# A fused retention and SoLU kernel: new instruction orders on every engine, and some casts and scales on other engines

## The chip, the cores and the metric

The kernel runs on one core of one Trainium2 chip. The metric is the device time of one execution, in microseconds (us). A profiled execution of the same program gives a trace with the start and duration of each instruction on each engine. PE is the engine that multiplies matrices, DVE the vector engine, ACT the scalar engine, POOL the GpSimd engine, and SP the engine that here only issues loads and stores.

## The reference

```python
# retention: q, k, v are (8, 8, 576, 64); B = batch, H = heads, S = positions, D = 64
scores = 1/sqrt(D) * q @ k^T
gamma = 1 - 2**(-5 - head);  Dmat = gamma**(i - j) where i >= j, else 0
attn = (scores * Dmat) @ v                      # (8, 8, 576, 64)
x = attn.transpose(0, 2, 1, 3).reshape(4608, 512)
# SoLU block: w_in (512, 1024), w_out (1024, 512), g_ln (1024)
h = x @ w_in
solu = h * softmax(h)
ln = (solu - mean) / sqrt(var + 1e-6) * g_ln
out = ln @ w_out                                # (4608, 512) float32
```

## The kernel before

The 576 positions of a batch are cut into two windows of 256 and a tail of 64. The tails of four batches make one window together, so there are 18 windows of 256 rows. A window is worked in two halves of four heads, which gives 36 steps `i` of retention, and in two tiles of 128 rows, which gives 36 tiles `t` of the SoLU block. Matrices are float16 on PE, sums float32.

A step `i` consists of these operations; the name of each is the letter(s) with the step's number:

- `ldq`, `ldk`, `ldv` (SP): the loads of 256 KB each; in the tails each is four transfers of 64 KB. There are five buffers for each of q, k and v.
- `sq`, `sk`: the scaling of q and k by powers of gamma, with the cast to float16 (`scale`, L394); `cv`: the cast of v (`cast_v`, L399). Each of these may stand on DVE, ACT or POOL, as the table `ON` says.
- `T` (PE): transposes of q and k (`qk_tp`, L419 wide, L429 in small tiles); `Te` or `TL` (ACT): their copy to SBUF (L455, L457). `TL` takes the transposes of step `i` together with those of an `L`.
- `K` (PE): k^T v of the step (`kv_mm`); `st` (DVE), `sm` and `sc` (POOL, L562 and L571): the running state of a batch, its decay and its cast.
- `S` (PE): the scores (`scores`, L508), into PSUM bank `s`; `mask` (DVE, L540).
- `I` (PE): the part of the output that comes from the state (`inter`); `V` (PE): the part from the masked scores (`av`); both into bank `xy`, L472. `xe` (ACT, L576): the copy to x.

A tile `t` consists of `M1` (PE, x @ w_in, L587, into bank `h`), `ex` (ACT, exp, L595), `so` (DVE, the product h * e, which frees bank `h`, L610), `bnA`, `bnB` (DVE, the variance), `fx` (ACT) and `rs` (POOL, 1/sqrt for a window, L650), `L` (PE, transposes of the product, L439 wide, L446 small), `Le` or `TL` (ACT), `M2` (PE, times w_out, L660), `oe` (ACT, the scaled result, L669, which frees the bank of `M2`, mostly `s`) and `out` (SP, the store). There are three buffers between `oe` and `out`. PE's steady group is `I L T V K S M1 M2`, each with its own number; the `M2` in it is four tiles behind the `M1`.

The weights come in eight transfers of 512 KB: `lwi0` to `lwi3` for w_in, cast in halves by `wi0a` to `wi3b` (L706), and `lwo0`, `lwo2`, `lwo4`, `lwo6` for w_out, scaled by g_ln in `wg0` to `wg7` (DVE L710, ACT L714). `WM` (PE, L720) makes the column means of all eight scaled blocks, after which `wc0` to `wc7` (DVE, L728) subtract them. `M2_0` needs all `wc`.

The order of the work is written out by hand. The tables `FIRST` and `LAST` list, for each engine, the operations of the first some twenty steps and of the last few; in between, an operation's place on its engine comes from a due time, its period (4.92 us a step) plus an offset. `order_ops` merges the engines' lists into one program order with the durations of `DUR`; each engine works through its own list strictly in turn and waits at the head of it. SP's list is a queue too: a store that waits for its `oe` holds the loads that stand behind it. Each transfer also waits until the one eight before it is complete.

Where the plan leaves PE idle before `M2_0`, `fill` puts in matmuls on zeros (L846) that keep it busy: 33 of them in this kernel, beside 12 at the start.

```python
q = o.name[0] in "VKSTL" and not wide(o.name)
x += 0.1 if q != quad else 0.0     # a change between small and whole tiles on PE
```

Of the kernel before, what the change touches and what calls it, by code (L numbers as in the profile page):

```python
# [9 lines left out]
FP = mybir.dt.float32  # L10
# [3 lines left out]
P = 128  # L14
# [3 lines left out]
for _b in range(0, B, 4):  # L18
# [5 lines left out]
    T=0.26, L=0.26, Tw=0.45, Lw=0.45, I=0.22, V=0.23, K=0.13, S=0.22, M1=1.73, M2=1.73, M2h=0.87, oeh=0.42, G=0.1, WM=1.73,  # L24
    TL=1.03, Te=0.58, Le=0.58, xe=0.74, ex=1.22, oe=0.69, va=1.25, wiA=0.62, wiB=0.45, wg=0.68, wgD=0.43,
    cvA=0.62, mask=1.22, st=0.58, so=1.22, soA=1.3, bnA=0.68, bnB=0.89, fx=0.2, fin=0.42, wc=0.74, wm=0.62,
    sqD=0.75, gc=0.17, cvD=0.45, sq=1.04, sk=1.04, cv=0.61, sm=0.42, sc=0.81, rs=0.69, rsB=1.0,
    ldx=0.88, ldw=1.36, out=0.65,
)
HOP, PE_OUT = 0.07, 0.2  # L30
# [4 lines left out]
ON = {'sq0': 'DVE', 'sq1': 'DVE', 'cv0': 'ACT', 'cv1': 'ACT', 'sk2': 'DVE', 'sk3': 'DVE', 'cv2': 'ACT', 'cv3': 'ACT', 'cv4': 'ACT', 'cv5': 'ACT', 'cv6': 'ACT', 'cv7': 'ACT'}  # L35
CAP = dict(
    rawq=5, rawk=5, rawv=5, q16=3, k16=4, v16=4, ev=8, s=1, ret=2, xy=1, gg=6, gt=2, s160=4, s161=9, h=1,
    e=2, solu=4, osb=3, tl=1, tlx=2, tlT=1, tlL=1, wst=5,
# [3 lines left out]
FIRST = dict(  # L42
    PE=(
# [5 lines left out]
    ),  # L49
    ACT=(  # L50
# [4 lines left out]
    ),  # L55
    DVE=(
# [5 lines left out]
    ),  # L62
    POOL=(
# [4 lines left out]
    ),  # L68
    SP=(
# [47 lines left out]
def wide(name):  # L117

    return name[0] == "T" and int(name[1:]) < NJ + 2 or name[0] == "L" and int(name[1:]) < NJ - 4


def plan():
    ops = []
    rank = {n: x - 1e4 for lst in FIRST.values() for x, n in enumerate(lst.split())}
    rank.update({n: x + 1e4 for lst in LAST.values() for x, n in enumerate(lst.split())})

# [5 lines left out]
    for i in range(NS):  # L132
# [32 lines left out]
    for t in range(NT):
# [5 lines left out]
        op(f"so{t}", "DVE", "soA" if va else "so", [f"ex{t}"], (m, 4.56), [("solu", [f"L{t}", f"va{t}" if va else f"bnB{t}"])])  # L171
# [5 lines left out]
        if c:  # L177
# [6 lines left out]
        after = [f"Te{NJ + 1}", f"Le{t - 1}"] if t == NJ - 4 else [f"TL{NS - 3}"] if t + 4 == NS - 2 else []  # L184
        after += [f"Le{t - 2}"] if t - 2 >= NS - 6 else []
        op(f"L{t}", "PE", "Lw" if early else "L", [f"so{t}"] + after, (m + 2, 0.1),
           [("tlL" if early else "tl" if jn else "tlx", [ev_L(t)])])
        if not jn:
# [3 lines left out]
        op(f"M2_{t}", "PE", "M2h" if end else "M2", need, (t + LAG, 3.1), [("h" if end else "xy" if late(t) and t % 2 else "s", [f"oe{t}"])])  # L192
# [5 lines left out]
    for c in range(4):  # L198
        op(f"lwi{c}", "SP", 0.47, [], (-4, 0.5 + 0.1 * c), [("wst", [f"wi{c}a", f"wi{c}b"])], DUR["ldw"])
        op(f"wi{c}a", "ACT", dict(ACT="wiA", DVE="wiB"), [f"lwi{c}"], (1, 0.1 * c))  # L200
        op(f"wi{c}b", "DVE", dict(ACT="wiA", DVE="wiB"), [f"lwi{c}"], (1, 0.1 * c))
    for c in range(0, 8, 2):
        op(f"lwo{c}", "SP", 0.47, [], (-2, 0.6 + 0.1 * c), [("wst", [f"wc{c}", f"wc{c + 1}"])], DUR["ldw"])
        for x in (c, c + 1):
            op(f"wg{x}", "DVE" if x % 2 else "ACT", dict(DVE="wgD", ACT="wg"), [f"lwo{c}", "gc"], (1, 1.0 + 0.1 * x))
            op(f"wc{x}", "DVE", "wc", ["wm" if WE else "WM", f"lwo{c}"], (4, 0.1 * x))
    op("G", "PE", "G", [], (-9999, 0.0), [("h", ["gc"])])
# [15 lines left out]
def parts(name):  # L223

    if name[:2] == "lw":
        return 1
    n = int(name[3:])
    if WINS[n // 2][1] == 2:
        return 2 if name[:3] == "out" else 4
# [731 lines left out]
```

## Time and profile before

| | us |
|---|---|
| median of 3 runs (lowest, highest) | 212.61 (212.51, 213.25) |
| span of the profiled execution, first to last instruction | 210.9 |
| PE busy, with the matmuls on zeros | 200.8 |
| DVE busy | 166.1 |
| ACT busy, POOL busy | 141.7, 141.7 |

Of the profiled execution's own time only the span is given; what lies around the span, up to the runs' median, is 1.7 us. In a row of the timeline the first number is the start, the second the duration, then engine, line, operation, the tensors written and read, shapes and count; in brackets stands the idle time of the engine just before, and what ended it. In a table of stretches each engine has its busy time and instruction count, followed by the granted clock of PE, the busy share of the DMA engines and the rate. A row of a group has the busy time and the mean duration in ns behind the first bar, and the idle time before its instructions behind the second.

### The profile page before, as it was taken

What the parts mean: (1) busy time and instruction counts of PE and PEld (TensorE: products, weight loads), DVE (VectorE), ACT (ScalarE), POOL (GpSimd) and SP (SyncE); (2) the same over time, 40 slices, a digit from 0 to 9 for tenths busy, and PEclk for the clock granted to TensorE, in tenths of its full rate; (3) what the DMA queues carried; (4) which work ended last, traced back from release to release, by engine and by line L of the source; (5) the groups of instructions that cost most, each with busy time, mean ns of one, the idle gap of its engine ahead of it and who ended that gap; (6) DMA issues with size and microseconds to landing.
All of it is one profiled execution on the core that took longest, in us unless ns stands there. A gap on an engine that the chain in (4) does not pass through costs nothing. (4 is left out here: it accounts for less than half of the span.)

```text
span 210.9 us, 10171 instructions
## 1 busy us (share of the span) xinstructions
PE 200.8 (95%) x4400; PEld 113.2 (54%) x4400; DVE 166.1 (79%) x279; ACT 141.7 (67%) x235; POOL 141.7 (67%) x240
## 2 busy tenths in 40 slices
PE   7986989999999999999999999999999999999992
PEld 2442654665566555555555555555666555554451
DVE  6565779997868898978898898889988998753760
ACT  2375787897666776776666777666767777573752
POOL 7434758999997975948787979797979792001110
PEclk9999999999999999999999999999999999999999
DMA  5999999999666559778999686776355222311224
GB/s 157 345 355 334 329 311 269 301 293 306 195 188 188 169 139 278 217 214 259 314 288 305 198 252 183 217 234 181 94 152 153 54 57 67 71 63 54 101 101 104
DMA packets 64814, 42.66 MB, mean 202 GB/s; under 512 B 3320, under 2 KB 58624, under 8 KB 64768
## 3 DMA queue, kind: packets, MB, share of 16 engines
q1 hardware_dynamic: 64528, 41.82, 68.4%
q8 instruction: 34, 0.56, 1.2%
q10 hardware_dynamic: 240, 0.18, 0.5%
q14 instruction: 12, 0.10, 0.2%
HBM read 32.55 MB, written 9.44 MB: 199 GB/s over the span
## 5 line engine op out<-in xcount | busy, mean ns | idle before, releaser
L587 PE MATMUL h_ps<-w_in,xT 128*128 128x512 f16 x288 | 68.5, 380 | 0.0
L660 PE MATMUL o_ps<-w2c,ev 128*128 128x512 f16 (+1 forms) x296 | 67.6, 373 | 0.0
L610 DVE TENSOR_TENSOR solu<-h_ps,e_sb 128x1024 f16<-128x1024 f32 x32 | 39.2, 1223 | 16.7 <-ACT e_sb L595 16.5
L595 ACT ACTIVATE e_sb<-h_ps 128x1024 f32<-128x1024 f32 x36 | 36.8, 1023 | 21.9 <-PE h_ps L587 20.4
L540 DVE TENSOR_TENSOR ret<-s_ps,masks 128x1024 f16<-128x1024 f32 x36 | 43.9, 1220 | 6.0 <-PE s_ps L508 5.4
L660 PEld LDWEIGHTS <-ev 128*128 128x128 f16 x296 | 28.7, 98 | 32.7
L616 DVE BATCH_NORM_STATS2 bs<-solu 128x6 f32<-128x512 f16 x64 | 43.6, 685 | 0.9
L587 PEld LDWEIGHTS <-xT 128*128 128x128 f16 x288 | 25.3, 98 | 29.1 <-ACT xT L576 0.8
L394 POOL TENSOR_TENSOR q<-rawq,small 128x512 f16<-128x512 f32 x34 | 35.4, 1042 | 7.3 <-DMA rawq<-in_q_dram 5.9
L669 ACT ACTIVATE o_sb<-o_ps,rs 128x512 f32<-128x512 f32 (+1 forms) x37 | 25.0, 676 | 21.8 <-PE o_ps L660 10.4
L394 POOL TENSOR_TENSOR k<-rawk,small 128x512 f16<-128x512 f32 x34 | 35.4, 1042 | 6.0 <-DMA rawk<-in_k_dram 5.9
L457 ACT COPY ev<-tl 128x1024 f32<-128x1024 f32 (+1 forms) x32 | 29.7, 932 | 4.7 <-PE tl L429 4.2
L576 ACT CAST xT<-xy 128x512 f16<-128x512 f32 x36 | 26.7, 742 | 3.0 <-PE xy L472 2.9
L571 POOL CAST sbd<-gg 64x256 f16<-64x256 f32 x64 | 25.4, 397 | 3.0
L562 POOL TENSOR_TENSOR gg<-gt,small 128x128 f32<-128x128 f32 x32 | 13.1, 409 | 16.9 <-DVE gt L557 16.5
L648 POOL TENSOR_TENSOR w<-mv,w 128x2 f32<-128x2 f32 x16 | 3.1, 194 | 27.8 <-ACT w L633 13.9
L399 POOL CAST v<-rawv 128x512 f16<-128x512 f32 x28 | 17.1, 609 | 0.2
L508 PE MATMUL s_ps<-ev 64*64 64x128 f16 x576 | 14.8, 218 | 0.3
L472 PE MATMUL xy<-ret,v 64*64 64x128 f16 x576 | 14.7, 217 | 0.0
L472 PEld LDWEIGHTS <-sbd 128*128 128x128 f16 x128 | 9.3, 98 | 9.3 <-issue 1.1
L446 PE MATMUL tl<-ident,solu 64*64 64x64 f16 x1024 | 14.2, 195 | 0.0
L846 PE MATMUL tl<-zeros 128*128 128x512 f16 x41 | 12.7, 445 | 1.3 <-DVE zeros L802 1.3
(71 smaller groups left out, 214.6 us busy)
## 6 DMA issues: line engine op xcount, KB each, us to landing
rawq<-in_q_dram SPq DMA_DIRECT2D x32, 256.0 KB, 5.1
rawk<-in_k_dram SPq DMA_DIRECT2D x32, 256.0 KB, 5.3
rawv<-in_v_dram SPq DMA_DIRECT2D x32, 256.0 KB, 5.1
out_dram<-o_sb SPq DMA_DIRECT2D x26, 256.0 KB, 3.1
out_dram<-o_sb SPq DMA_DIRECT2D x19, 128.0 KB, 2.3
wst<-in_moe_w_in_dram SPq DMA_DIRECT2D x4, 512.0 KB, 6.8
wst<-in_moe_w_out_dram SPq DMA_DIRECT2D x4, 512.0 KB, 7.1
rawq<-in_q_dram SPq DMA_DIRECT2D x16, 64.0 KB, 2.4
```

The lines of the kernel that those rows point to most:

```text
L394: eng.tensor_tensor(out=t.rearrange("p j h d -> p h j d"), in0=st[i]["r" + nm], in1=g, op=ALU.mult)
L457: nc.scalar.copy(out=t[:, lo:hi].rearrange("p x (r w) -> p r x w", r=2), in_=tls[n].rearrange("p r x w -> p (r x w)").bitcast(FP).rearrang ...
L472: nc.tensor.matmul(start=(c, e) not in begun, stop=False, skip_group_check=True, **kw)
L540: nc.vector.tensor_tensor(out=d["ret"].rearrange("p e h j q -> p (e h) (j q)"), in0=d["s"].rearrange("p e h j q -> p (e h) (j q)"), in1=ma ...
L571: nc.gpsimd.tensor_copy(out=t[ee[e], :, :, ee[e]], in_=st[i]["gg"][ee[e]])
L576: nc.scalar.copy(out=xT[:, 2 * w : 2 * w + 2, 2 * hf : 2 * hf + 2].rearrange("p c h (q j) -> p c h j q", j=2), in_=xys[i][:, :, 0:256].rea ...
L587: nc.tensor.matmul(out=h_ps[:, hh], lhsT=xT[:, t, dc], rhs=w_in16[:, dc, hh], start=(dc == 0), stop=(dc == 3),)
L595: nc.scalar.activation(out=d["e"], in_=d["h"], func=ACT.Exp, accum_out=se[:, t : t + 1])
L610: nc.vector.tensor_tensor(out=d["solu"], in0=d["h"], in1=d["e"], op=ALU.mult)
L616: nc.vector.bn_stats(out=d["bs"][:, half], in_=d["solu"][:, half * 512 : half * 512 + 512])
L660: nc.tensor.matmul(out=o, lhsT=d["ev"][:, d["lo"] + c], rhs=w2c16[:, c, mm], start=(c == 0), stop=(c == 7))
L669: nc.scalar.activation(out=d["osb"][:, mm], in_=d["o", half], func=ACT.Copy, scale=ws[t // 2]["rs"][:, t % 2 : t % 2 + 1])
```

## The change

The change does four things that reach the program.

1. `FIRST` and `LAST` go; a table `ORDER` lists all operations of all engines from the first to the last step. The planner's durations, its load queue and its rule for DVE and POOL at the same time are other ones, and by them the merged program order and the place of the matmuls on zeros (34 instead of 33).
2. `ON` moves operations: `sk0 sq2 sq3 sq4 sk6 cv9 sq11 cv11` from POOL to DVE; `sq1 sk3` from DVE to POOL; `cv1 cv3 cv4 cv6` from ACT to POOL; `cv14` from POOL to ACT; of the weights `wi0a wi1a wi2a` from ACT to POOL, `wi3a wg0 wg4` from ACT to DVE, `wi1b wg5 wg7` from DVE to ACT.
3. On SP the loads and stores have another order. Of the first 34 transfers the same ones stand in places 1 to 25 and 26 to 34, but inside them `lwo0` goes from the 18th place to the 25th and `ldv6` from the 25th to the 19th. Later, loads run ahead of their numbers, and some stores behind later ones (`out3 ldk17 ldq17 out2 out4`, `out13 out12`, `out19 ldq31 ldq35 out18`, `out25 out23 out24`).
4. On PE every step keeps its operations and the same ones stand ahead of `M1_4`, but `I V K L T S` change places within a group. `L2` comes before `T9`.

Small: the table of constants has 94 columns instead of 78; the buffers of the weights are a pool of their own at the end. The diff also brings transposes by DMA, split loads, a second bank for the end and extra load buffers, but their switches (`LX`, `TX`, `R0`, `OT`, `SPL`) are set so that none of them is used.

```diff
-HOP, PE_OUT = 0.07, 0.2
+HOP, PE_OUT = 0.04, 0.2
...
-ON = {'sq0': 'DVE', 'sq1': 'DVE', 'cv0': 'ACT', 'cv1': 'ACT', 'sk2': 'DVE', 'sk3': 'DVE', 'cv2': 'ACT', 'cv3': 'ACT', 'cv4': 'ACT', 'cv5': 'ACT', 'cv6': 'ACT', 'cv7': 'ACT'}
+ON = {'sq0': 'DVE', 'sq1': 'POOL', 'cv0': 'ACT', 'cv1': 'POOL', 'sk2': 'DVE', 'sk3': 'POOL', 'cv2': 'ACT', 'cv3': 'POOL', 'cv4': 'POOL', 'cv5': 'ACT', 'cv6': 'POOL', 'cv7': 'ACT', 'sk0': 'DVE', 'wi3a': 'DVE', 'sq2': 'DVE', 'sq3': 'DVE', 'sq4': 'DVE', 'sk6': 'DVE', 'wg4': 'DVE', 'wg0': 'DVE', 'cv9': 'DVE', 'sq11': 'DVE', 'cv11': 'DVE', 'wi1b': 'ACT', 'wg5': 'ACT', 'wg7': 'ACT', 'cv14': 'ACT', 'wi1a': 'POOL', 'wi0a': 'POOL', 'wi2a': 'POOL'}
...
+LX = ()
+TX = ()
+R0 = 99
+OT = 99
+SPL = ()
...
-FIRST = dict(
+ORDER = dict(
     PE=(
-        "T0 S0 K0 K1 T1 I0 S1 V0 I1 V1 M1_0 K2 T2 T3 K3 S2 M1_1 I2 S3 V2 L0 I3 V3 T4 L1 K4 S4 M1_2 K6 WM K5 "
-        "M1_3 T5 K7 T6 I4 S5 V4 T7 I5 S6 V5 T8 M1_4 I6 S7 V6 K8 T9 L2 M2_0 I7 L3 V7 K9 S8 M1_5 M2_1 I8 L4 V8 "
-        "K10 S9 T10 M1_6 M2_2 I9 L5 V9 S10 K11 T11 M1_7 M2_3 I10 L6 V10 S11 K12 T12 M1_8 M2_4 I11 L7 T13 V11 "
...
+        "G T0 K0 K1 S0 T1 S1 I0 V0 I1 V1 M1_0 K2 T2 S2 T3 M1_1 K3 S3 T4 I2 V2 L0 I3 V3 S4 K4 M1_2 K6 L1 WM K5 M1_3 T5 K7  "
+        "S5 T6 I4 V4 T7 I5 V5 S6 T8 M1_4 I6 S7 V6 K8 L2 T9 M2_0 I7 L3 V7 S8 K9 M1_5 M2_1 I8 V8 L4 K10 T10 S9 M1_6 M2_2  "
+        "I9 V9 K11 L5 T11 S10 M1_7 M2_3 I10 V10 K12 L6 T12 S11 M1_8 M2_4 I11 L7 V11 K13 T13 S12 M1_9 M2_5 I12 V12 L8 T14  "
...
     DVE=(
-        "wg3 mask4 st6 so2 st5 wc4 wc0 wc7 wc1 st7 so3 mask5 wc5 wc2 wc6 mask6 wc3 mask7 fin0 st8 so4 mask8 "
-        "st9 bnA4 fin1 so5 bnA5 mask9 bnB4 st10 so6 bnB5 mask10 st11 so7 bnA7 mask11 bnB7 st12 bnA6 so8 "
...
+        "sk0 sq0 gc st0 mask0 st1 mask1 wi3b wi0b wi3a wi2b sk2 sq2 sq3 so0 st2 mask2 sq4 st3 mask3 so1 sk6 wg4 st4  "
+        "mask4 wg3 wg1 wg0 st6 so2 wc1 st5 wc0 wc2 wc3 st7 wc6 mask5 so3 wc5 wc4 mask6 wc7 mask7 st8 fin0 cv9 so4 fin1  "
+        "mask8 st9 sq11 bnA4 so5 cv11 mask9 st10 bnA5 so6 bnB5 mask10 st11 bnA6 so7 bnB4 mask11 bnA7 st12 so8 bnB7  "
...
     POOL=(
-        "sk0 sk1 sm0 sc0 sm1 sc1 sq2 sq3 sm2 sc2 sm3 sc3 sk4 sq4 sk6 sm4 sc4 sk5 sm6 sk7 sm5 sq5 sc5 sq6 sq7 "
-        "sk8 sq8 sk9 sc6 cv8 sq9 sm7 sc7 rs0 sq10 cv9 sq11 sm8 cv11 sk10 sc8 cv10 sk11 rs1 sm9 sc9 sq12 sm10 "
...
+        "sk1 cv1 sq1 sm0 sc0 sm1 sc1 wi1a wi0a wi2a sk3 cv3 sm2 sk4 sc2 sm3 sc3 cv4 cv6 sm4 sc4 sk5 sm6 sk7 sq5 sm5 sc5  "
+        "sq6 sq7 sk8 sq8 sc6 cv8 sq9 sk9 sm7 sc7 rs0 sm8 sc8 sk10 cv10 sq10 sm9 sc9 sq12 sk11 sm10 rs1 sq13 cv12 sc10  "
...
     SP=(
-        "ldq0 ldk0 ldv0 ldv1 ldq1 ldk1 lwi1 lwi2 lwi0 lwi3 ldk2 ldv2 ldq2 ldk3 ldq3 ldv3 lwo4 lwo0 ldk4 ldq4 "
-        "ldv4 lwo6 ldk6 lwo2 ldv6 ldk5 ldv5 ldk7 ldq5 ldv7 ldq6 ldk8 ldq7 ldq8 ldk9 ldv8 ldq9 ldq10 ldv9 "
...
+        "ldk0 ldq0 ldk1 ldv0 ldv1 ldq1 lwi3 lwi1 lwi0 lwi2 ldk2 ldv2 ldq2 ldq3 ldk3 ldv3 ldk4 ldq4 ldv6 ldv4 lwo4 ldk6  "
+        "lwo6 lwo2 lwo0 ldk5 ldv5 ldk7 ldq5 ldv7 ldq6 ldq7 ldk8 ldq8 ldv8 ldq9 ldk9 ldv9 ldq10 ldv11 ldv10 ldk10 ldq12  "
+        "ldq11 ldq13 out0 ldk11 ldk12 ldq14 ldq16 ldv12 ldq15 ldv14 ldv13 ldv15 out1 ldv16 ldk13 ldk14 ldk15 out3 ldk17  "
+        "ldq17 out2 out4 ldk16 out5 ldq20 ldv18 ldk18 ldk19 out6 ldk20 ldq21 ldq19 ldk21 ldv17 ldq18 ldv20 out7 ldv19  "
...
-    rank = {n: x - 1e4 for lst in FIRST.values() for x, n in enumerate(lst.split())}
-    rank.update({n: x + 1e4 for lst in LAST.values() for x, n in enumerate(lst.split())})
+    rank = {n: x for lst in ORDER.values() for x, n in enumerate(lst.split())}
...
-        t = max(free[o.eng], lock if o.eng == "POOL" else free["POOL"] if locks(o) else 0.0)
+        t = free[o.eng]
...
         if locks(o):
+            if free["POOL"] > x + 0.05:
+                end += 0.2
+                free["POOL"] += 0.18
             lock = end
+        elif o.eng == "POOL" and lock > x + 0.05:
+            end += 0.18
...
+            u = units(o.name) / np
             for _ in range(np):
-                end = max([end + o.dur / np] + landed[-7:-6])
+                begin, end = end, end + o.dur / np
+                held += u
+                while held > 5.0:
+                    held -= landed[out_at][1]
+                    end = max(end, landed[out_at][0] - 0.2)
+                    out_at += 1
```

More of the change, by code (lines that the diff above doesn't have):

```diff
@@ L183, in plan @@
         early = t < NJ - 4
[L184 to L188, printed above, removed]
+        if t in LX:
+            op(f"lx{t}", "SP", "lx", [f"so{t}"], (m + 2, 0.1), [("ev", [f"M2_{t}"])], DUR["ltx"])
+        lasts = [x for x in range(NT) if NJ - 4 <= x < OT and ev_L(x)[:2] == "Le"]
+        after = [f"Te{NJ + 1}", f"Le{NJ - 5}"] if t == NJ - 4 else []
+        if t in lasts:
+            after += [f"Le{t - 2}" if t - 2 in lasts else ev_T(max(i for i in range(NS) if i not in TX))]
+        if t not in LX:
+            op(f"L{t}", "PE", "Lw" if wide(f"L{t}") else "L", [f"so{t}"] + after, (m + 2, 0.1),
+               [("tlL" if early else "o2" if t >= OT else "tl" if jn else "tlx", [ev_L(t)])])
+        if ev_L(t)[:2] == "Le":
             op(f"Le{t}", "ACT", "Le", [f"L{t}"], (m + 2, 0.95), [("ev", [f"M2_{t}", "M3" if t == NT - 1 else ""])])
@@ L191, in plan @@
         need = [ev_L(t)] + [f"wc{x}" for x in range(8)] + ["cs" if t == NT - 2 else ""]
-        op(f"M2_{t}", "PE", "M2h" if end else "M2", need, (t + LAG, 3.1), [("h" if end else "xy" if late(t) and t % 2 else "s", [f"oe{t}"])])
+        if t == OT:
+            need += [ev_T(max(x for x in range(NS) if x not in TX)), ev_L(max(x for x in range(OT) if x not in LX))]
+        op(f"M2_{t}", "PE", "M2h" if end else "M2", need, (t + LAG, 3.1), [(home(t), [f"oe{t}"])])
         op(f"oe{t}", "ACT", "oeh" if end else "oe", [f"M2_{t}", f"rs{w}"], (t + LAG + 1, 0.1), [("osb", [f"out{t}"])])
@@ L223, in parts @@
 def parts(name):
-    if name[:2] == "lw":
+    if name[:2] in ("lw", "lx"):
         return 1
+    if name[:2] == "tx":
+        return 2
     n = int(name[3:])
+    if name[:2] == "ld" and split(n) and name[2] != "q":
+        return 4
     if WINS[n // 2][1] == 2:
@@ L230, in parts, with units @@
     return 2 if name[:3] == "out" and 22 <= n < 28 else 1
+def units(name):
+    if name[:3] == "out":
+        return 0.25
+    if name[:2] in ("lw", "lx", "tx"):
+        return dict(lw=0.5, lx=2.0, tx=4.0)[name[:2]]
+    return 2.0 if split(int(name[3:])) and name[2] != "q" else 1.0
 def order_ops(ops):
@@ L303, in _np_table @@
         st[64 * (h % 2) : 64 * (h % 2) + 64, h // 2] = gam[h] ** 256.0
-    small = np.concatenate(cols + [st, np.ones((P, 1)), np.full((P, 1), -0.5), np.eye(P, 8)], 1)
+    pos_s = 128 * (p[:, None] // 64) + 64 * j[None] + p[:, None] % 64
+    ks = (gam[None, :, None] ** (128.0 - pos_s[:, None, :])).reshape(P, 16)
+    small = np.concatenate(cols + [st, np.ones((P, 1)), np.full((P, 1), -0.5), np.eye(P, 8), ks], 1)
     return small.astype(np.float32)
@@ L339 @@
     pool("raw", CAP["rawq"])
-    for name in ("q16", "k16", "v16", "ev", "ret", "gg", "gt", "e", "solu", "osb", "wst"):
+    for name in ("q16", "k16", "v16", "ev", "ret", "gg", "gt", "e", "solu", "osb"):
         pool(name, CAP[name])
@@ L376, in load @@
         hh = slice(4 * hf, 4 * hf + 4)
-        st[i]["r" + nm] = t = pools["raw"].tile([P, 4, 2, D], FP, tag=nm, name="raw" + nm)
-        if wi < 2:
+        if extra(i) and "bis" not in pools:
+            loads_w.close()
+            pool("bis", CAP["bisq"])
+        st[i]["r" + nm] = t = pools["bis" if extra(i) else "raw"].tile([P, 4, 2, D], FP, tag=nm, name="raw" + nm)
+        if split(i) and nm != "q":
+            for n in range(4):
+                r0 = 256 * wi + 64 * n
+                nc.sync.dma_start(
+                    out=t[64 * (n // 2) : 64 * (n // 2) + 64, :, n % 2],
+                    in_=src[b, hh, r0 : r0 + 64, :].rearrange("h p d -> p h d"),
+                )
+        elif wi < 2:
             nc.sync.dma_start(
@@ L400, in cast_v, with bank @@
         st[i]["v16"] = t
+    def bank():
+        if "o2" not in pools:
+            banks_2.close()
+            pool("o2", CAP["o2"], space=PS)
+        return pools["o2"].tile([P, 512], FP, tag="o2", name="o_ps")
     def tl_of(n):
@@ L503, in scores @@
         qT, kT = qk_of(i, 0), qk_of(i, 1)
+        sz = s_ps.rearrange("p e h j q -> p e h (j q)")
         for hp in range(2):
@@ L507, in scores @@
                     for e in range(2):
+                        half = split(i) and j
+                        qq = slice(64 * c + 32, 64 * c + 64) if half else ee[c]
+                        oo = sz[ee[c], e, hp, 128:192] if half else sv[ee[c], e, hp, j]
                         nc.tensor.matmul(
-                            out=sv[ee[c], e, hp, j], lhsT=kT[ee[e], hp, j, ee[c]],
-                            rhs=qT[ee[e], hp, :, ee[c]], start=True, stop=True,
+                            out=oo, lhsT=kT[ee[e], hp, j, ee[c]], rhs=qT[ee[e], hp, :, qq], start=True, stop=True
                         )
@@ L654, in mm2 @@
         d = tk[t]
-        nm = "xy" if half or late(t) and t % 2 else "s"
-        nm = "h" if t == NT - 1 and not half else nm
+        nm = "xy" if half else home(t)
         mm = slice(256 * half, 256 * half + (256 if t == NT - 1 else DM))
-        d["o", half] = o = pools[nm].tile([P, 2, 512], FP, tag=nm, name="o_ps")[:, 0, 0 : mm.stop - mm.start]
+        o = bank() if nm == "o2" else pools[nm].tile([P, 2, 512], FP, tag=nm, name="o_ps")[:, 0]
+        d["o", half] = o = o[:, 0 : mm.stop - mm.start]
         for c in range(8):
@@ L867 @@
                 emit(o)
+    if "bis" not in pools:
+        loads_w.close()
+    pool("gu", 1)
     def general(t):
```

167 lines of the change are left out of this document (103 added, 64 removed), and 48 rows, old and new, of tables (ACT, DVE, PE, POOL).

## The prediction

> **What bounds the kernel now.** I read the head of the page first, then the table of stretches, then the timeline of the engines around the one place where the stretches change character.
>
> ```profile
> span 210.9 us, 10171 instructions
> PE 200.8 (95%) x4400; PEld 113.2 (54%) x4400; DVE 166.1 (79%) x279; ACT 141.7 (67%) x235; POOL 141.7 (67%) x240
> ```
>
> The profiled execution's span is 210.9 us; the median of the runs is 212.61, so 1.7 us lie around the span, and I carry every difference over to 212.61 unchanged. Half a per cent, about what a measurement of this kernel can tell from no change, is 1.06 us.
>
> ```profile
> core 0: us, PE busy (x) PEld busy (x) DVE busy (x) ACT busy (x) POOL busy (x), PEclk, DMA share, GB/s
> 20.00:25.00 5.00, 4.09 (x89) 2.60 (x88) 3.68 (x8) 3.38 (x6) 3.93 (x8) 1.00 1.14 336
> 30.00:35.00 5.00, 4.49 (x51) 2.03 (x50) 4.75 (x11) 3.86 (x7) 3.92 (x8) 1.00 1.07 280
> 35.00:41.00 6.00, 5.31 (x118) 3.42 (x117) 5.68 (x11) 5.22 (x12) 5.86 (x8) 1.00 1.08 289
> 41.00:60.00 19.00, 18.68 (x419) 11.37 (x418) 16.36 (x29) 14.83 (x24) 18.38 (x29) 1.00 0.96 262
> 60.00:95.00 35.00, 35.00 (x894) 20.31 (x893) 29.68 (x46) 24.61 (x41) 26.12 (x44) 1.00 0.68 198
> 95.00:115.00 20.00, 19.69 (x528) 11.50 (x527) 17.40 (x28) 13.62 (x21) 16.82 (x28) 1.00 0.98 294
> 115.00:180.00 65.00, 65.00 (x1678) 37.41 (x1677) 58.29 (x91) 45.60 (x73) 51.35 (x86) 1.00 0.56 155
> ```
>
> Two regimes. From 41 us on PE has work without a break (35.00 of 35, 65.00 of 65), so an order can win there only what is hidden in the small gaps. Before 41 us the load queue is full (DMA share above 1) and PE waits; part of its busy time is warm-up matmuls on zeros. The border is `M1_4`, at 41.33. Since the change puts the same PE operations ahead of `M1_4` and the same ones behind it, only in another order, the time is: when `M1_4` starts, plus a fixed amount of PE work, plus gaps. What sets `M1_4`?
>
> ```profile
> 33.26 1.04 POOL L394 TENSOR_TENSOR k<-rawk,small 128x512 f16<-128x512 f32 x1 [0.22 <-DMA rawk<-in_k_dram]
> 34.50 0.40 POOL L562 TENSOR_TENSOR gg<-gt,small 128x128 f32<-128x128 f32 x1 [0.20 <-DVE gt L557]
> 34.86 1.04 POOL L394 TENSOR_TENSOR q<-rawq,small 128x512 f16<-128x512 f32 x1
> 35.84 0.85 POOL L571 CAST sbd<-gg 64x256 f16<-64x256 f32 x2
> 36.77 2.04 POOL L394 TENSOR_TENSOR q<-rawq,small 128x512 f16<-128x512 f32 x2
> 39.77 1.04 POOL L394 TENSOR_TENSOR q<-rawq,small 128x512 f16<-128x512 f32 x1
> ...
> 40.87 0.40 PE L419 MATMUL tl<-ident,q 128*128 128x128 f16 x4
> ...
> 41.33 1.90 PE L587 MATMUL h_ps<-w_in,xT 128*128 128x512 f16 x8
> ```
>
> POOL runs `sk7` (after the 28th load), `sm5`, `sq5`, `sc5`, `sq6`, `sq7`, `sk8`, `sq8` without a pause, `sq8` ends at 40.81, `T8` starts at 40.87 and `M1_4` right behind it. So: 28th load, POOL's chain, PE.
>
> **The start of `M1_4`.** The changed load order has the same 28 transfers ahead of `ldq5`, the 29th, and a saturated queue delivers by bytes; so `sk7` may again start at 33.26 and end at 34.30. The changed POOL list goes on with `sq5 sm5 sc5 sq6 sq7 sk8 sq8`: 5 x 1.04 + 0.40 + 0.85 and about 0.1 of starts = 6.55, from 34.30 (or about 34.45, if `ldq5` itself comes just after that): `sq8` ends at 40.85 to 41.0. That is 0.0 to +0.2 against 40.81; I take **+0.1**. Everything that the change does earlier must pass this gate. The seven operations that leave ACT in the first 35 us (16 casts and scalings before, 9 after), and the scales that change between POOL and DVE, let `M1_1` and `M1_2` start sooner (0.69 on DVE instead of 1.04 on POOL for a scale, the group rows below), but that head start is waited away, unless the gate itself moves.
>
> ```profile
> L394 POOL TENSOR_TENSOR q<-rawq,small 128x512 f16<-128x512 f32 x34 | 35.4, 1042 | 7.3 <-DMA rawq<-in_q_dram 5.9 <-PE tl L429 0.5
> L394 DVE TENSOR_TENSOR q<-rawq,small 128x512 f16<-128x512 f32 x2 | 1.4, 692 | 0.9 <-DMA rawq<-in_q_dram 0.9
> L399 POOL CAST v<-rawv 128x512 f16<-128x512 f32 x28 | 17.1, 609 | 0.2
> L706 DVE CAST w_in<-wst 128x512 f16<-128x512 f32 x4 | 1.6, 420 | 0.9 <-DMA wst<-in_moe_w_in_dram 0.9
> ```
>
> A second way into the same gate is the weight chain, and the change lengthens it: `lwo0` moves from the 18th to the 25th transfer, and behind it DVE must run `wg1` and `wg0` before PE's `WM`. In the trace the 25th transfer is `ldv6`:
>
> ```profile
> 30.68 0.62 ACT L399 CAST v<-rawv 128x512 f16<-128x512 f32 x1 [0.21 <-DMA rawv<-in_v_dram]
> ...
> 31.60 1.90 PE L720 MATMUL tl<-w2c,minus 128*128 128x512 f16 x8
> 33.43 0.32 PE L472 MATMUL kv<-v,k 64*64 64x64 f16 x16
> ...
> 28.89 1.94 DVE L710 TENSOR_SCALAR w2c<-wst,gln 128x512 f16<-128x512 f32 x3
> 28.43 1.04 POOL L394 TENSOR_TENSOR k<-rawk,small 128x512 f16<-128x512 f32 x1 [1.89 <-DMA rawk<-in_k_dram]
> 29.43 0.58 POOL L562 TENSOR_TENSOR gg<-gt,small 128x128 f32<-128x128 f32 x1
> 31.64 1.04 POOL L394 TENSOR_TENSOR k<-rawk,small 128x512 f16<-128x512 f32 x1 [0.55 <-DMA rawk<-in_k_dram]
> ```
>
> With 30.68 for `lwo0`, two scalings at 0.42 (row L706, nearest in size and form) to 0.65 each (the three of 28.89 took 1.94) let `WM` start at 31.6 to 32.0; before it was 31.60. Behind `WM` (1.83 to `K5`) come K5, then `wc1` and `st5` on DVE, then POOL's `sm5`. `sm5` must not come later than the end of `sq5`, 35.35 to 35.5. `WM` at w gives `wc1` at w + 1.93, `st5` about 0.7 later and 0.6 long, `sm5` at w + 3.25: the limit is w = 32.2. So this chain has 0.2 to 0.6 us of slack and costs nothing in the forecast.
>
> The scales newly on DVE stand beside POOL work, and the trace shows what that costs: the first of the three at 28.89, beside `sk6`, and POOL's 0.58 instead of 0.40 right after. By the nearest rows a meeting costs 0.0 to 0.45 on DVE and about 0.2 on POOL. [...]
>
> **The gaps after `M1_4`.** Those that I find by going through PE's starts:
>
> ```profile
> 44.34 0.40 PE L419 MATMUL tl<-ident,q 128*128 128x128 f16 x4 [0.19 <-POOL q L394]
> ...
> 57.17 0.69 ACT L669 ACTIVATE o_sb<-o_ps,rs 128x512 f32<-128x512 f32 x1 [0.67 <-PE o_ps L660]
> ...
> 57.38 0.40 PE L472 MATMUL xy<-ret,v 64*64 64x128 f16 x16
> 57.91 0.42 PE L508 MATMUL s_ps<-ev 64*64 64x128 f16 x16
> ...
> 102.66 0.19 PE L429 MATMUL tl<-ident,q 64*64 64x64 f16 x1
> 103.17 0.31 PE L429 MATMUL tl<-ident,q 64*64 64x64 f16 x15 [0.31 <-issue]
> ...
> 98.04 0.40 PE L472 MATMUL xy<-ret,v 64*64 64x128 f16 x16
> 98.27 0.29 PE L472 MATMUL xy<-v,k 64*64 64x64 f16 x16
> 98.39 0.40 PE L508 MATMUL s_ps<-ev 64*64 64x128 f16 x16
> ```
>
> - `T9` waits 0.19 for `sq9`. In the changed order `L2` stands ahead of `T9`, eight matmuls of the shape of `T8` (0.46, 40.87 to 41.33), and POOL's `sk9` ends at about 44.5 (40.95 + 0.85 + 0.61 + 2 x 1.04 for `sc6 cv8 sq9 sk9`), before `T9` would start: **-0.2**.
> - `S10` starts 0.53 after `V9`, where 0.23 is the pace of a V (98.04 to 98.27). It needs bank `s`, which `oe2` (57.17 to 57.86) holds. The new order puts `K11 L5 T11` in front of `S10`: **-0.3**. In the same way I allow **-0.2** for smaller waits of about 0.1 at other `S`.
> - `T20` loses 0.5 between its first and second matmul to "issue", not to an operation. No order removes that by intent; the loads around it are laid out otherwise. Between 0 and -0.5, and as much could appear elsewhere: **-0.2**.
> - Permuting V, K, T and S costs nothing: the pace is that of each operation (V 0.23, K 0.12), with one change into and one out of the small tiles in both orders. I allow +-0.01 for each of 31 groups, +-0.3 in all.
> - DVE, already busy 16.36 of 19 in 41 to 60, gets `cv9`, `sq11` and `cv11` (0.42 + 0.69 + 0.42, about 1.5), and pays by deferring `bnB4`; ACT gets one cast, `cv14`. New small waits, 0 to 0.6: **+0.2** (the lower half, since DVE had 2.6 us free there).
>
> The last 25 us have the same order on PE, without gaps before and after; `oe31` and `oe30` swap on ACT behind no wait of PE's. Nothing.
>
> Sum: +0.1 - 0.2 - 0.3 - 0.2 - 0.2 + 0.2 = -0.6; 212.61 - 0.6 = **212.0**. With all bounds at their good end -1.6 (211.0), at their bad end about +0.8 (213.4).
>
> **The rivals.** [...]
>
> *The gate opens earlier* (faster). The 29th load lands a place sooner, because ready slots and a queue without holes deliver it so, or POOL's chain closes up, and the issue gaps do not return: 212.0 - 0.8 - 0.3 = **210.9**. For it: seven operations fewer on ACT and earlier `M1_1`, `M1_2`. Against: a queue at a share above 1 has no holes to close.
>
> *A store is held back.*
>
> ```profile
> 63.49 2.77 SPq L384 DMA_DIRECT2D rawk<-in_k_dram  x4
> ...
> 72.49 0.69 ACT L669 ACTIVATE o_sb<-o_ps,rs 128x512 f32<-128x512 f32 x1 [0.61 <-PE o_ps L660]
> ```
>
> `out2` moves behind `out3` and two four-part loads: from `oe3`'s end, about 63, plus 2 x 2.77 it issues near 68.6 and must land before `oe5` (72.49) can have its buffer, three being there. If it lands after that, `oe5`, bank `s` and the next `S` wait: +0 to +1, **212.5**. That the change does nothing that can be measured is contained in the forecast.
>
> **How the numbers follow.** Forecast 0.52 (211.0 to 213.4), weight chain 0.20, earlier gate 0.18, held store 0.10. Faster than 211.55: all of the earlier gate and 0.3 of the forecast, 0.34. Slower than 213.67: three quarters of the weight chain and a little of the held store and the forecast, 0.18. Within: 0.48. The range takes in the rivals at their prices: 210.8 to 213.9, which leaves about 1 in 10 out at each end.
>
> **What would show it.** Right: `M1_4` at 41.3 to 41.6, `WM` before 32.2, no "POOL q" wait at `T9`, `S10` right behind `T11`, PE busy 35.00 of 35 and 65.00 of 65 again. Wrong: `M1_4` off by more than 0.5 either way; a wait of ACT's `o_sb` for a store; PE gaps in 41 to 60 above the 0.3 there are.

## The result, and the profile after

The changed kernel took 214.91 us (median of 22 runs, 213.29 to 221.63) beside 213.05 us for the kernel before (22 runs, 212.35 to 214.57) on the same chip: ratio 1.0065, 95% interval 1.0040 to 1.0089, so slower by 0.9 to 1.9 us. The forecast was 212.0, within 210.8 to 213.9. Ratios here and below leave out every run more than 1.5% above the fastest of its kernel (five of the 22 here; with all runs the median is 1.86 us higher). The runs of the changed kernel also lie much further apart than those of the kernel before.

First the head of the page and the same table of stretches as in the prediction, for the changed kernel (span 215.3 us, its run 217.06, so a run from the upper part):

```profile
span 215.3 us, 10127 instructions
```

```profile
35.00:41.00 6.00, 4.62 (x113) 3.13 (x113) 5.60 (x11) 4.60 (x10) 5.81 (x9) 1.00 1.08 286
41.00:60.00 19.00, 19.00 (x421) 11.58 (x421) 17.38 (x30) 14.36 (x24) 16.83 (x27) 1.00 0.83 224
60.00:95.00 35.00, 32.59 (x816) 18.71 (x814) 26.98 (x42) 23.25 (x39) 26.32 (x43) 1.00 0.82 236
95.00:115.00 20.00, 19.77 (x511) 11.57 (x511) 17.08 (x29) 13.62 (x22) 15.81 (x26) 1.00 0.82 241
115.00:180.00 65.00, 64.15 (x1667) 37.25 (x1658) 54.28 (x87) 44.64 (x73) 50.33 (x88) 1.00 0.53 153
```

41 to 60 is better than before (19.00 of 19, before 18.68), as forecast. The loss begins at 60: 2.41 us of PE missing in 60 to 95 and 0.85 in 115 to 180, where before there was none. The timeline of PE, POOL and SP around the largest hole:

```profile
77.84 0.30 PE L515 MATMUL tl<-ident,k 64*64 64x64 f16 x16
80.34 0.32 PE L575 MATMUL xy<-v,k 64*64 64x64 f16 x16 [2.20 <-POOL v L478]
...
72.28 0.85 POOL L692 CAST sbd<-gg 64x256 f16<-64x256 f32 x2
76.21 2.04 POOL L473 TENSOR_TENSOR k<-rawk,small 128x512 f16<-128x512 f32 x2 [3.09 <-DMA rawk<-in_k_dram]
...
79.12 1.17 POOL L478 CAST v<-rawv 128x512 f16<-128x512 f32 x2
...
70.57 0.90 SPq L801 DMA_DIRECT2D out_dram<-o_sb  x2
71.57 1.95 SPq L463 DMA_DIRECT2D rawk<-in_k_dram  x4
```

`K15` waits 2.20 us for `cv15`. Its load had long landed, but POOL's list has `sk16 sk17 rs3 cv16` ahead of it, and `sk16` waited 3.09 us for `ldk16`, a load in four parts that SP issued only at 71.57, behind `out3 ldk17 ldq17 out2 out4`. The other holes are of another kind. The list of PE's waits from 60 to 200 us (who waits for whom: total us, times, longest; PEld is PE's loading of weights), first before, then after:

```profile
PEld L446 <- issue: 1.3, 3, 0.4
PEld L429 <- issue: 0.4, 1, 0.4
PE tl L429 <- issue: 0.3, 1, 0.3
```

```profile
PEld L575 <- issue: 2.7, 2, 2.3
PE xy L575 <- POOL v L478: 2.2, 1, 2.2
PEld L534 <- issue: 1.8, 4, 0.9
PE tl L534 <- issue: 1.0, 2, 0.8
PE xy L575 <- issue: 0.2, 1, 0.2
```

The 2.3 us of the first row lie at the same `K15`. Beside this one wait for POOL there are stops that no operation causes ("issue"). By PE's starts they cost about 2.1 us in this profile and 0.7 before.

### The profile page after: what moved, and what is told of

Read it like the earlier page. It is cut to its first block, busy times and chain, and to the rows that moved or that the text cites. A ratio compares the mean times of both kernels' runs of the same rounds, so it can differ in the third digit from the quotient of the medians.

```text
span 215.3 us, 10127 instructions
## 1 busy us (share of the span) xinstructions
PE 202.7 (94%) x4401; PEld 114.1 (53%) x4401; DVE 169.3 (79%) x285; ACT 137.6 (64%) x229; POOL 140.6 (65%) x240
## 5 line engine op out<-in xcount | busy, mean ns | idle before, releaser
L737 DVE BATCH_NORM_STATS2 bs<-solu 128x6 f32<-128x512 f16 x64 | 43.0, 680 | 0.2
L473 POOL TENSOR_TENSOR k<-rawk,small 128x512 f16<-128x512 f32 x33 | 34.3, 1047 | 12.1 <-DMA rawk<-in_k_dram 11.5
L473 POOL TENSOR_TENSOR q<-rawq,small 128x512 f16<-128x512 f32 x31 | 32.2, 1041 | 1.5 <-DMA rawq<-in_q_dram 0.8
L973 PE MATMUL tl<-zeros 128*128 128x512 f16 x45 | 14.5, 447 | 1.3 <-DVE zeros L929 1.3
```

Source lines behind the costliest of these rows:

```text
L473: eng.tensor_tensor(out=t.rearrange("p j h d -> p h j d"), in0=st[i]["r" + nm], in1=g, op=ALU.mult)
L737: nc.vector.bn_stats(out=d["bs"][:, half], in_=d["solu"][:, half * 512 : half * 512 + 512])
```

## The experiments

In each, "ratio" is that to the kernel before, run beside it on the same chip, with its 95% interval.

**1. Which part of the program?** Four kernels. `a0_after` is the changed kernel again.

> The changed kernel again, for another profile. Every theory expects the ratio to before found already, 1.004 to 1.009 (+0.9 to +1.9 us), and M1_4 within 0.3 us of before's. The theory that the loads and stores out of number order are at fault (call it the middle) expects the lost time between 60 and 120 us, in waits of PE for a cast or scale on POOL whose POOL list was held by a load; the place may differ from the first profile, because it takes any lateness of the queue. The rival that one fixed spot is at fault (K15 waiting for cv15) expects the same 2.2 us at the same K15.

`x3_sp_pool`: SP behind `ldq8` and POOL behind `sq8` as before.

> The changed kernel with the loads and stores behind ldq8 and POOL's operations behind sq8 back in the order of before (rs7 and later three places later, so that the order closes); PE, DVE and ACT as changed. The middle theory (SP and POOL orders cost the time): -0.6 to +0.2 us to before, ratio 0.997 to 1.001, and runs that scatter no more than before's. The rival that the orders of PE, DVE and ACT cost it, or that POOL's and PE's orders no longer fit: +0.9 to +1.9 us as the changed kernel, or more.

`x4_start`: only the start is changed.

```diff
 # each engine: changed list up to M1_4 / ldq8 / sq8 / xe5 / mask7, then the list of before
-ON: 'cv9': 'DVE', 'sq11': 'DVE', 'cv11': 'DVE', 'cv14': 'ACT'
```

> The changed kernel up to M1_4, ldq8, sq8, xe5 and mask7; every later operation in the order of before and with cv9, sq11, cv11 and cv14 back on POOL. The middle theory: -0.5 to +0.2 us to before (M1_4 at 41.3 to 41.5). The rival that the new start costs the time later, by the state in which it leaves the load queue: +0.9 to +1.9 us.

`x5_middle`: only what follows the start is changed.

> The reverse: the order and the engines of before up to M1_4, ldq8, sq8, xe5 and mask7, everything later as changed (39 matmuls on zeros instead of 34). The middle theory: +0.9 to +2.5 us to before, with a wider scatter than before's runs. The rival that the new start costs the time: -0.5 to +0.3 us.

Measured: `a0_after` 1.0148 (1.0098 to 1.0198), `x4_start` 1.0024 (1.0000 to 1.0048), `x5_middle` 1.0149 (1.0104 to 1.0195). So the changed kernel's loss lies in the main behind the start; the start alone adds 0 to 1.0 us. One thing limits what follows: the changed kernel came out at 1.0065 (1.0040 to 1.0089) in the first comparison and at 1.0148 (1.0098 to 1.0198) in this one, and the intervals do not meet. In the second profile of the changed kernel `K15` waits again, and pays more (timeline of PE, then a row of the table of stretches):

```profile
80.53 0.32 PE L575 MATMUL xy<-v,k 64*64 64x64 f16 x16 [2.45 <-POOL v L478]
...
81.08 3.46 PE L708 MATMUL h_ps<-w_in,xT 128*128 128x512 f16 x8
```

```profile
82.00:84.00 2.00, 2.00 (x6) 0.67 (x5) 1.72 (x5) 0.00 (x0) 2.00 (x3) 0.50 1.00 292
```

Behind 2.45 us of idling the granted clock (third column from the right in the row of the stretch) is 0.50, and `M1_11` takes 3.46 us instead of 1.90. After the 2.20 us of the first profile the clock stayed at 1.00. The profile of `x5_middle`, with the same lists on POOL and SP there, has no wait at `K15` at all: `sk16` waited 0.65 us for `ldk16` instead of 3.09. So this wait comes and goes from run to run.

`x3_sp_pool` came out at 1.0771 (1.0719 to 1.0824), far from both expectations. By its waits the POOL list and the changed DVE list don't fit: POOL's 1/sqrt (`rs`) wait for the variances that DVE now does later, and hold the scales behind them.

```profile
POOL w L768 <- DVE mv L738: 37.0, 9, 8.0
...
PEld L514 <- POOL q L472: 3.6, 2, 3.0
```

It tells how closely the lists are tied, not which of them is at fault.

**2. Is it the wait at `K15`?** One operation moved on POOL, one load on SP, both, and both with PE's old order.

```diff
 POOL  -sk16 sk17 rs3 cv16 cv15      +cv15 sk16 sk17 rs3 cv16           # y1
 SP    -ldk17 ldq17 out2 out4 ldk16  +ldk16 ldk17 ldq17 out2 out4       # y2; y3 has both
 PE    behind M2_8: I V L K S T and the like  ->  I L T V K S           # y4, with both moves
```

> The changed kernel with one operation moved on POOL: cv15 ahead of sk16 instead of behind sk16 sk17 rs3 cv16. Theory A (K15's wait for cv15, held behind sk16 whose load ldk16 is issued late, is what the median pays): the 2.2 to 2.45 us wait at K15 is gone, and with it the lower granted clock behind it; -1.5 to -3 us against the changed kernel, that is 0 to +1 us to before. Theory B (PE's stops marked issue, 1.2 to 2.1 us in the changed kernel's profiles against 0.5 before, are the main part): still +0.9 to +1.9 us to before, with L16 to V20 and the like as long as they were.

> The changed kernel with one load moved on SP: ldk16 ahead of ldk17 and ldq17 instead of behind ldk17 ldq17 out2 out4. Theory A: sk16 starts right behind sc13 at about 73.2 instead of 76.2 to 76.4, cv15 ends by 77.3, K15 does not wait: 0 to +1 us to before. The rival that POOL's order and not the load is at fault: K15 waits as long as before, +0.9 to +1.9 us. Theory B: K15's wait may go, but +0.9 us or more remain in stops marked issue.

> Both moves. Theory A: as the better of the two, 0 to +1 us to before, and no run above 216. Theory B: +0.9 to +1.9 us.

> Both moves, and PE in the order of before behind M2_8 (I L T V K S in every group); the other engines as changed. If the changed order of V, L, K, T and S itself costs PE time: the steps from M1_23 to M1_29 lose the 0.06 to 0.16 us each that the changed kernel shows there (0.5 in all), so -0.5 to -0.7 us to the kernel with both moves. If it costs nothing (as the prediction has it, within 0.3): the same time within 0.3 us.

Measured: `y1_cv15` 1.0050 (0.9996 to 1.0105), `y2_ldk16` 1.0115 (1.0060 to 1.0170), `y3_both` 1.0069 (1.0033 to 1.0104), `y4_pe` 1.0055 (1.0022 to 1.0088). No profile of the four has a wait at `K15` for `cv15`, and `y2`, `y3` and `y4` are still slower than before, clear of noise (`y1` is not resolved). So the wait is not the whole loss. What share it has is open: beside 1.0065 the four are no better than the changed kernel, beside 1.0148 `y4` is. Nor is it all that the worst runs pay. The two profiles that have it are of runs of 217.06 and 218.78 us; but `cv15` no longer stands behind `sk16` in `y1` and `y3`, and ten of their 24 runs still took more than 216 us. Of `y4`, run beside them, none of 12 did (the highest 215.69), nor any of the 24 of `z2_middle` and `f4_z2_few` below, which have the same three repairs. So it looks as if the high runs go with PE's changed order; no profile is of such a run of `y1` or `y3`, and it is not shown.

`y4_pe` shows one piece of it. In its profile the steps from `M1_23` to `M1_29` last as long as before; in the profiles with the changed PE order five of these six steps last 0.06 to 0.16 us longer, 0.47 in all. (In time, `y3` to `y4`, so little is not resolved.) One group each in PE's timeline, before and after:

```profile
142.31 0.27 PE L472 MATMUL xy<-ev,sbd 128*128 128x128 f16 x2
...
143.05 0.41 PE L472 MATMUL xy<-ret,v 64*64 64x128 f16 x16
143.27 0.31 PE L472 MATMUL xy<-v,k 64*64 64x64 f16 x16
143.40 0.41 PE L508 MATMUL s_ps<-ev 64*64 64x128 f16 x16
143.74 0.39 PE L587 MATMUL h_ps<-w_in,xT 128*128 128x512 f16 x1
```

```profile
145.50 0.28 PE L575 MATMUL xy<-ev,sbd 128*128 128x128 f16 x2
...
146.20 0.31 PE L575 MATMUL xy<-v,k 64*64 64x64 f16 x16
146.44 0.42 PE L615 MATMUL s_ps<-ev 64*64 64x128 f16 x16
...
147.04 0.39 PE L708 MATMUL h_ps<-w_in,xT 128*128 128x512 f16 x1
```

From `I26` to `M1_24` it is 1.43 us before and 1.54 after. `K` to `S` is 0.13 before, behind `V`, and 0.24 after, behind `L`: the same small matmuls, at another pace.

**3. The groups, the loads of the start, the end.** `z1_groups` is the kernel before with PE's changed order from `M1_4` to `M1_13` only; `s1_sp34` is `x4_start` with the first 34 loads as before; `z2_middle` is `x5_middle` with the three repairs of `y4_pe`; `t1_end` is `z2_middle` with ACT behind `ex30` and DVE behind `so30` as before.

> The kernel before with PE's groups from M1_4 to M1_13 in the changed order (L2 ahead of T9, S behind L and T); all other orders and engines of before (39 matmuls on zeros). If step 3 of the prediction is right for these groups: the waits at T9, S9, S10 and S11 go, -0.4 to -0.7 us to before. If their gain is taken back by a wait of V, K or T for another engine: -0.2 to +0.3 us.

> The kernel x4 (changed start, everything behind M1_4 as before) with the first 34 loads in the order of before, lwo0 in the 18th place again; casts and scales stay where the change put them (41 matmuls on zeros). If the order of the loads makes the 28th load late (33.9 on average in the profiles of the changed start, against 33.2): M1_4 at 41.0 to 41.5 and -0.3 to +0.2 us to before. If the new places of the casts and scales make the queue late: M1_4 at 41.7 or later and +0.3 to +1 us.

> The kernel x5 (start of before, middle and end as changed) with three things put right: cv15 ahead of sk16, ldk16 ahead of ldk17, and PE in the order of before behind M2_8. If K15's wait, the steps of PE's order behind M1_23 and the start were the whole loss: -0.5 to +0.3 us to before. If the end (the last stores, some 0.7 us later behind oz in every profile of the changed end) and stops marked issue remain: +0.4 to +1.2 us.

> As z2_middle, with ACT behind ex30 and DVE behind so30 in the order of before too. If the order of these two engines makes the last stores late: the stretch from oz's start to the end of the span falls from 4.9 to 4.2 us and the time by 0.7 us against z2_middle. If it is only where an instruction transfer of 16 KB falls: the stretch stays at 4.8 to 5.0 us as long as such a transfer lies in the last 4 us, whatever the order.

Measured: `z1_groups` 1.0033 (1.0002 to 1.0063), `s1_sp34` 1.0131 (1.0076 to 1.0186), `z2_middle` 1.0044 (1.0012 to 1.0075), `t1_end` 1.0149 (1.0093 to 1.0205). In its profile `z1_groups` gains what it should: `M1_4` starts 0.24 and `M1_12` 0.94 us before those of the kernel before, so the groups bring 0.70. `oz`, the last piece of ACT, starts 0.93 earlier. But the span is 210.9 us, as before: the end takes it back, though every order there is that of before. `t1_end` has the slow end too (`oz` at 208.82, span 213.9), and a wait of its own making: PE waits 1.5 us for `mask` on DVE behind `M1_31`. `s1_sp34` has `M1_4` at 43.30: the old load order with the new casts is later still, which does not tell what makes the new one late. `z2_middle` at 1.0044 beside `x5_middle` at 1.0149 says more: the intervals lie apart, so the three repairs together (`cv15`, `ldk16`, PE's order) take back some 2 us of what the changed middle loses. Which of the three does it, these runs do not tell.

**4. The end.** Only the number of matmuls on zeros at the very start is changed.

```diff
-fill(tl1[1].bitcast(FP), 12)
+fill(tl1[1].bitcast(FP), 18)      # f2, on the kernel before
+fill(tl1[1].bitcast(FP), 4)       # f1 on the changed kernel, f3 on z1_groups, f4 on z2_middle
```

> The kernel before with 18 instead of 12 matmuls on zeros at its start, that is 12 more instructions on PE and nothing else. If the end depends on where PE's instruction transfers of 16 KB fall: such a transfer appears in the last 4 us, the stretch from oz's start to the end of the span grows from 4.15 to about 5.0, and the time by 0.5 to 0.9 us (ratio 1.002 to 1.004). If the end depends on the orders: 4.15 us stays and the time is the same within 0.3 us.

> The changed kernel with 4 instead of 12 matmuls on zeros at its start, 16 fewer instructions on PE. By the first theory (place of the instruction transfers) the end falls from 4.9 to 4.2 us and the time by 0.5 to 0.9 us against the changed kernel, if 16 instructions are enough; the waits in the middle stay. By the second (orders) the end stays at 4.9 us.

> The kernel z1 (before, with PE's groups from M1_4 to M1_13 in the changed order) with 4 instead of 12 matmuls on zeros at its start, so 4 instructions fewer on PE than the kernel before. First theory: the end at 4.2 us, oz at 205.8 to 206.2, and -0.3 to -1.0 us to before. Second: as z1, +0.3 to +0.8 us.

> The kernel z2 (start of before; middle and end as changed, with cv15 and ldk16 moved and PE in the order of before behind M2_8) with 4 instead of 12 matmuls on zeros at its start. First theory: the end at 4.2 us and -0.7 to +0.3 us to before, so the rest of the changed middle costs nothing. Second: as z2, +0.3 to +1.6 us.

ACT's last instruction, `oz`, in the timeline of the kernel before and of `f2_before_more`:

```profile
206.75 0.47 ACT L669 ACTIVATE o_sb<-o_ps,rs 128x256 f32<-128x256 f32 x1 [0.41 <-PEq L916]
```

```profile
207.12 0.47 ACT L669 ACTIVATE o_sb<-o_ps,rs 128x256 f32<-128x256 f32 x1 [0.41 <-PEq L916]
```

The spans are 210.9 and 212.2 us, so from `oz` to the end it is 4.15 us before and 5.08 in `f2_before_more`. The instruction queues in the last 5 us of each (packets, MB, share of 16 engines):

```profile
q14 instruction: 3, 0.02, 1.8%
```

```profile
q8 instruction: 1, 0.02, 1.1%
q14 instruction: 2, 0.02, 0.9%
```

Six more matmuls at the start, with their six weight loads, and one transfer of 16 KB on the queue `q8` falls among the last stores. The store that ACT issues there takes 1.0 us longer from issue to landing (last number), in the same stretches:

```profile
out_dram<-o_sb ACTq DMA_DIRECT2D x1, 128.0 KB, 2.4
```

```profile
out_dram<-o_sb ACTq DMA_DIRECT2D x1, 128.0 KB, 3.4
```

Over the whole execution, from the page of each:

```profile
q8 instruction: 34, 0.56, 1.2%
```

```profile
q8 instruction: 35, 0.57, 1.1%
```

So there is a 35th transfer. In the trace they have 16 KB each and come about every 5 us, the last ones 10 to 12 us apart; that they are PE's follows from the change of PE's instructions alone. All 18 profiles divide in this way: the five without such a transfer in their last 4 us (the kernel before, `x4_start`, `f1`, `f3`, `f4`) take 4.07 to 4.27 us from `oz` to the end, the thirteen with it 4.80 to 5.42. The changed kernel has 35, but with 16 instructions fewer (`f1_after_few`) 34, and `x4_start`, with the same 4401 matmuls and as many weight loads, has 34 too. Why the last stores take longer beside a transfer that comes when PE is done, no run shows.

In time: `f2_before_more` 1.0050 (1.0018 to 1.0082), of which the profile puts 0.93 us on the end and 0.37 on what lies ahead of `oz`. `f3_z1_few` **0.9944 (0.9907 to 0.9981)**, median 211.98 against 212.73: faster than both kernels. `f4_z2_few` 1.0031 (0.9999 to 1.0063) and `f1_after_few` 1.0073 (1.0033 to 1.0112): their profiles have the short end (4.07 and 4.26 us), but their times are not resolved from those of `z2_middle` and the changed kernel. From `z1_groups` to `f3_z1_few`, each against the kernel before beside it, it is 0.9 to 2.9 us (worked out from the two ratios and their intervals), so the 1.0 of the end may be all of it or a part.

## Why the prediction was wrong

Four steps failed: the start of `M1_4` (forecast +0.1), the stops marked "issue" (-0.2), the permuting on PE (0) and the last 25 us (0) all came out dearer. And no step priced a load that stands late on SP. The gains in the groups came as forecast. By its own steps:

- **The start of `M1_4`: +0.1.** In the profile of the changed kernel it is 41.37 against 41.33, right on the forecast, and by the second way that the prediction names: `sk7` started at 32.86, 0.40 early, and `sq5` then waited for `ldq5` until 34.43.

```profile
32.86 1.04 POOL L473 TENSOR_TENSOR k<-rawk,small 128x512 f16<-128x512 f32 x1 [0.31 <-DMA rawk<-in_k_dram]
34.43 1.04 POOL L473 TENSOR_TENSOR q<-rawq,small 128x512 f16<-128x512 f32 x1 [0.53 <-DMA rawq<-in_q_dram]
```

  As a rule it is not: the nine profiles of kernels with the whole changed start have `M1_4` at 40.99 to 43.43, mean 42.06; the eight with the start of before, some with other numbers of matmuls on zeros, at 41.09 to 42.91, mean 41.60. So the term is about +0.5, as `x4_start` has it in time (0 to 1.0), and the scatter within each start is larger. The step that failed is the author's assumption "a saturated queue delivers by bytes", against which the rates below speak. POOL's chain follows without a pause once it has `sk7` and `sq5`, as described, but these start with the 28th and 29th load, and those come when they come. From 15 to 25 us, before, then `y4_pe` (the last two columns are the busy share of the DMA engines and GB/s), then `sk7` and `M1_4` in the timeline of `y4_pe`:

```profile
15.00:20.00 5.00, 4.18 (x40) 1.80 (x38) 2.36 (x6) 3.43 (x6) 1.09 (x2) 1.00 1.16 318
20.00:25.00 5.00, 4.09 (x89) 2.60 (x88) 3.68 (x8) 3.38 (x6) 3.93 (x8) 1.00 1.14 336
```

```profile
15.00:20.00 5.00, 3.52 (x36) 1.56 (x34) 3.01 (x6) 1.84 (x4) 0.22 (x1) 1.00 1.03 255
20.00:25.00 5.00, 4.73 (x94) 2.81 (x93) 4.81 (x9) 2.08 (x4) 4.62 (x8) 1.00 0.98 281
```

```profile
34.73 1.04 POOL L472 TENSOR_TENSOR k<-rawk,small 128x512 f16<-128x512 f32 x1 [0.30 <-DMA rawk<-in_k_dram]
...
42.66 0.59 PE L707 MATMUL h_ps<-w_in,xT 128*128 128x512 f16 x2
```

  The same 28 loads stand in front, at 255 and 281 GB/s instead of 318 and 336 (289 and 316 in the first profile of the changed kernel). What slows them is not settled, and the start of before can be late too: 42.91 in `f3`.

- **The weight chain: nothing.** Right: `WM` at 31.21 in the changed kernel. Where `WM` came as late as 32.96 (`y4_pe`), `sm5` still stood right behind `sq5`, for the loads had moved both. `wg1` and `wg0` ran from 30.11 to 30.99, ahead of `sk5` at 31.14, so they met no POOL scale. No run shows the price of a late weight chain that the upper end of the range, 213.9, takes in: of the four `wg` on DVE in this profile one starts inside a POOL operation, 0.33 us before its end, and takes 0.61 us, and the other three take 0.47 to 0.49. Scales met POOL elsewhere. Of the eight scales on DVE in this profile the five that start inside no POOL operation take 0.68 to 0.69 us; the three that start inside one take 0.96, 1.02 and 1.20, and each ends 0.54 to 0.55 us behind the end of that POOL operation. The longest:

```profile
49.68 1.04 POOL L473 TENSOR_TENSOR q<-rawq,small 128x512 f16<-128x512 f32 x1
...
50.08 1.20 DVE L473 TENSOR_TENSOR q<-rawq,small 128x512 f16<-128x512 f32 x1
```

  In the 18 profiles together 36 scales on DVE start more than 0.15 us before the end of a POOL operation, and all 36 end 0.54 to 0.55 us behind it. Here a meeting costs up to 0.51 us (1.20 against 0.69), a little over the 0.45 that the prediction allowed for a meeting.

- **`T9`, `S10` and the other `S`: -0.7.** Right, to the tenth: 0.70 in `z1_groups`, and 0.71 from `M1_4` to `M1_12` in `f3_z1_few`. In the changed kernel `T9` follows `L2` without a wait, and `S10` comes 0.29 behind `T11`:

```profile
44.11 0.62 PE L527 MATMUL tl<-ident,solu 128*128 128x128 f16 x8
44.56 0.22 PE L505 MATMUL tl<-ident,q 128*128 128x128 f16 x1
...
57.57 0.34 PE L515 MATMUL tl<-ident,q 64*64 64x64 f16 x16
...
57.86 0.41 PE L615 MATMUL s_ps<-ev 64*64 64x128 f16 x16
```

- **`T20`, stops marked "issue": -0.2.** They did not go. They are about 2.1, 1.6, 1.2 and 1.0 us in the four profiles that have all of the changed lists behind `M1_4` (the changed kernel twice, `x5`, `f1`), against 0.7 before, so wrong in sign there. That the change brings them is not shown: the list of `y2`, which differs from the changed kernel in one load, has no stop of PE's matmuls from 60 to 200 us, and that of `s1`, with the order of before behind `M1_4`, has 2.6 us of them.
- **Permuting `V`, `K`, `T` and `S`: 0, at most 0.3.** Under-sized: +0.47 behind `M1_23`, shown by `y4_pe`. The prediction gave each operation a pace of its own; in the group shown above `K` to `S` is 0.13 us with `V` in front and 0.24 with `L` in front.
- **DVE's extra work: +0.2.** Nothing: from 60 to 200 us PE waits for DVE nowhere, and 41 to 60 is full.
- **The last 25 us: nothing.** Wrong by +0.65 to +0.8 (4.80 and 4.97 us from `oz` to the end in the two profiles against 4.15). That the order on PE was the same was true and beside the point: a few of PE's instructions more or fewer, at the very start, lengthen or shorten this stretch (`f2` 5.08 us against 4.15, `f1` 4.26 against 4.80, `f3` 4.1 against 5.1 in `z1_groups`).
- **The rivals.** None took place. `oe5` started at 72.29, 0.04 us behind the last matmul of `M2_5`, and waited for no store. The start of `M1_4` did move, but later. "A store is held back" came nearest: it looked at the same run of transfers on SP, but at the stores in it and not at `ldk16` behind them. The price that was missed is that of a load which stands late on SP, ahead of which POOL may do nothing.
- **The bounds.** Those that the steps name add up to -1.5 at the good end (it has -1.6) and to +0.4 at the bad one, or +0.9 if another stop of 0.5 appears (it has about +0.8). Nothing hangs on this.

Without the wait at `K15` the terms are +0.5 (start), -0.7 (groups), +0.5 (PE's order) and +0.7 (end), +1.0 us in all, and with the stops of those four profiles (+0.3 to +1.4) +1.3 to +2.4. This is worked out from profiles of single runs, against 0.9 to 1.9 measured in the first comparison and 2.1 to 4.2 in the second. With the wait another 2.2 to 4 us come on top in some runs. The end is shown by changing it alone, in profile and time, and PE's order in the profile; what slows the loads of the start, what brings the stops and what makes the two comparisons differ stay open.

## What to carry to other kernels

When a change only reorders work around an engine that is already full, price first what the order is coupled to: an in-order list on one engine (POOL) whose head waits for an in-order list on another (SP) passes a late load on, as the 3.09 us for which `sk16` waited came out as 2.20 us at `K15`. A gain of 0.7 us in the middle counts only if the end is measured with it: take the last 5 us of both profiles and compare the DMA packets there, the instruction queue's too. And one profile is one draw: the start gate was on forecast in it, and 0.5 us late on average.

## What the runs showed of the hardware

Not expected: twelve more instructions on PE, 200 us earlier, make the stretch from `oz` to the end 0.93 us longer (5.08 in `f2_before_more`, 4.15 before), with one more 16 KB transfer of instructions among the last stores. A scale on DVE (0.69 us alone) that starts more than 0.15 us before the end of a POOL operation ends 0.54 to 0.55 us behind that end, 36 times of 36 in the 18 profiles.

And PE idling for 2.45 us once was followed by a granted clock of 0.50 for 3.4 us (`a0_after`; worked out from its means of 0.71, 0.50 and 0.86 in 80 to 82, 82 to 84 and 84 to 85 us), where 2.20 us in another run was not (1.00 from 80.3 to 84). The length of the idling alone does not decide it. In `x3_sp_pool` PE idled for 2.86 us, with the clock at 1.00 through and behind it (95 to 115 us):

```profile
98.17 0.32 PE L514 MATMUL tl<-ident,q 64*64 64x64 f16 x16 [2.86 <-POOL q L472]
```

In the same profile the clock fell to 0.50 at 127.4 us behind two waits of 0.46 and 0.68; its mean from 115 to 130 us is 0.91, and PE idled for 1.30 us in all there.
